# Other sizes of transfer at the layers' border, at the layers' last units and in w_down: two layers of cached attention and FFN on one core

## The chip, the core and the metric

The kernel runs on one core of a Trainium2 chip. The metric is the device time of one execution in microseconds, the median of several runs. A profile of one execution (engines, waits, DMA) goes with it.

The engines: PE multiplies matrices (its weight loads are told apart as PEld), DVE, ACT and POOL work on vectors, and SP issues all the loads here. Sixteen DMA engines move the data; each load is spread over all of them, and the loads of SP's queue are worked off in the order of their issue.

## What is computed

Twice, one after the other, an attention block and an FFN, each with a residual, for 4 rows of 512 (one new token in each of 4 sequences):

```python
def _A_ref(x, k_cache, v_cache, wq, wo):        # k_cache, v_cache: 4 x 8 x 8192 x 128
    q = (x @ wq).reshape(B, Sq, 32, 128).transpose(0, 2, 1, 3)
    k = jnp.repeat(k_cache, 4, axis=1)
    v = jnp.repeat(v_cache, 4, axis=1)
    p = softmax(jnp.einsum("bhqd,bhkd->bhqk", q, k) * 128 ** -0.5)
    o = jnp.einsum("bhqk,bhkd->bhqd", p, v)
    return o.transpose(0, 2, 1, 3).reshape(B, Sq, 32 * 128) @ wo

def _B_ref(x, w_gate, w_up, w_down):            # 512 x 1792, 512 x 1792, 1792 x 512
    return (silu(x @ w_gate) * (x @ w_up)) @ w_down

x = A_x
x = x + _A_ref(_layernorm(x), A_k_cache, A_v_cache, A_wq, A_wo)
x = x + _B_ref(_layernorm(x), B_w_gate, B_w_up, B_w_down)
x = x + _A_ref(_layernorm(x), A_k_cache, A_v_cache, A_wq, A_wo)
x = x + _B_ref(_layernorm(x), B_w_gate, B_w_up, B_w_down)
```

The caches are 64 MB each in bf16, and both layers read the same ones, so nearly all of the caches has to be fetched twice.

## The kernel before

**Units.** A unit is one of the 32 pairs of sequence and head group: a K and a V of 8192 x 128 in bf16, 2 MB each. They lie in `kv`, 8 slots of 2 MB in the on-chip memory (`kvf`, 128 partitions of 16 KB for a slot). A slot is used in eighths: `s6.3` is the name of the fourth 1024 columns of slot 6. For K an eighth is turned by DVE (`turn`) and multiplied on PE (`scores`, 4 matmuls); then the softmax, and `values` multiplies with V. The last unit of a layer has its V multiplied eighth by eighth (`block_last`, 8 matmuls each), all others in two blocks.

**Loads.** `items` is the order in which SP issues the loads; `pump` issues the next whenever its slot (`home`) is free. A usual unit is one DMA of 2 MB. Some units are loaded in quarters of 512 KB (`fours`, `part`): the last unit of each layer, whose V has a semaphore for each quarter (`split`, `sem_l`), and three units of layer 1 that come right behind the border. K and V of a unit have the same pieces, since the piece sets which keys lie in which partition. The last three units of layer 0 stay in their slots and are the first of layer 1.

**Border of the layers.** The FFN weights go where slots 6 and 7 were: `f0` is the first column of slot 6, then three pieces of w_gate (5376 columns), then w_down from `f1` (14 rows of blocks, `fo` = 0 to 13, of 512 columns each), then the last pieces of w_gate and w_up. The other pieces of w_up have room of their own. In the FFN of layer 0, the room of weights that were read is given to the K of two units of layer 1 (`ks[0]` into slot 6, `ks[1]` into slot 7), quarter by quarter: two quarters behind the gate matmuls, the others in the loop over `fo`, as soon as `fo` passes the quarter's end, and the last ones behind the loop. Then `heirs`: two of the kept K units hand their slots on, a quarter at a time, as their scores go on (`quarter`, called from `keys` and `finished`).

**Who waits for what.** There is no compiler that finds dependencies. Each instruction states names that it reads and writes, and `_Sync` keeps for each name its last writer and its readers (`_need`, `_record`, lines 42 to 93). A reader waits for the last writer of each name; a writer waits for the readers as well. For DMAs the writer is the semaphore that tells of the landing. For the weights, `at_w` gives the names: the eighths of slots 6 and 7 that the columns touch (`room`), and the block's own name.

```python
room = lambda a, b: places[(a - f0) // (TB * Dh):(b - 1 - f0) // (TB * Dh) + 1]
at_w = {"wg": room(f0, f0 + FR * F), "wg3": room(f2, f2 + F), "wu": room(f3, f3 + F),
        **{("wd", j): room(f1 + 2 * j * D, f1 + (2 * j + 2) * D) + [f"wd{j}"] for j in range(FO // 2)}}
```

**FFN.** `ffn` multiplies gate and up (56 matmuls each, the weights stationary, `w_sb[kt][:, f:f + 2 * P - 1:2]`: every second column), makes `hT` on DVE and ACT, then w_down. w_down is loaded in 7 blocks of 256 KB, two `fo` in each: a block is laid out so that a partition holds two neighbouring rows, and so gate and up take every second column. In layer 0 the w_down weights are stationary (4 matmuls for each `fo`, with a `warm` matmul before each pair, which does no needed work). In layer 1 `hT` is stationary and the weights stream (two matmuls for each `fo`), and nothing is given away. There the last load is w_down, behind the last V and w_gate; w_up and one piece of w_gate were kept from layer 0.

PE, DVE and ACT programs are taped first and then played with loops over the regular middle of each layer (`roll`); SP's is straight.

Of the kernel before, what the change touches and what calls it, by code (L numbers as in the profile page):

```python
# [146 lines left out]
def bass_interleave_layers__gqa_block_cached__swiglu_ffn__decode_kernel(  # L147
# [12 lines left out]
    B, _, D = A_x.shape  # L160
    _, G, S, Dh = A_k_cache.shape
# [4 lines left out]
    P = 128  # L166
    assert Dh == P and B * Hq == P and D % P == 0 and F % P == 0 and B == 4
    KT = D // P
    FO = F // P
# [23 lines left out]
    with ExitStack() as es:  # L193
# [16 lines left out]
        wg_sb = [kvf[:, a:a + F] for a in (f0, f0 + F, f0 + 2 * F, f2)]  # L210
        wu_sb.append(kvf[:, f3:f3 + F])
        wd_sb = kvf[:, f1:f1 + FO * D].rearrange("p (f n) -> p f n", f=FO)
        places = [f"s{s}.{q}" for s in range(NKEEP, NSLOT) for q in range(NB)]
        room = lambda a, b: places[(a - f0) // (TB * Dh):(b - 1 - f0) // (TB * Dh) + 1]
        at_w = {"wg": room(f0, f0 + FR * F), "wg3": room(f2, f2 + F), "wu": room(f3, f3 + F),
                **{("wd", j): room(f1 + 2 * j * D, f1 + (2 * j + 2) * D) + [f"wd{j}"] for j in range(FO // 2)}}
        wq_sb = sb("wq_sb", [P, KT, HqDh], BF16)
        wq_b = wq_sb[:].rearrange("p k n -> p (k n)").bitcast(U8)

# [43 lines left out]
        def few(ap):  # L263
# [10 lines left out]
        engines = {"pe": nc.tensor, "act": nc.scalar, "dve": nc.vector, "pool": nc.gpsimd, "sp": nc.sync}  # L274
        prog = {n: sem(f"prog_{n}") for n in engines}
        sem_s = [sem(f"sem_s{i}") for i in range(NSLOT)]
        sem_l = [sem(f"sem_l{q}") for q in range(NQ)]
        sem_h = [[sem(f"sem_h{k}{i}") for i in range(NQ)] for k in range(2)]
        sem_p = [sem(f"sem_p{i}") for i in range(7)]
        sem_x = sem("sem_x")  # L280
        sem_w = {n: [sem(f"sem_{n}{i}") for i in range(c)]
                 for n, c in (("wq", KT), ("wo", 1), ("wg", KT), ("wu", KT), ("wd", FO // 2))}
        sem_out = sem("sem_out")
        es.enter_context(nc.Block())
        T = _Sync(nc, engines, prog)
# [62 lines left out]
        split = {("V", L, unit_order[L][-1]) for L in range(2)}  # L348

        heirs = {("K", 1, unit_order[1][k]): items[ends[0] + 3 + k] for k in range(2)}  # L350
        fours = {(L, unit_order[L][-1]) for L in range(2)} | {(1, u) for u in unit_order[1][NRES:2 * NRES]}
        issued = [0]
        free = set(range(NSLOT))
        slot_of = {}
# [16 lines left out]
        def load_weight(name, i=0):  # L371
            if name == "wq":
                T.dma("sp", [(wq_sb[:, i, :], runs(A_wq[i * P:(i + 1) * P, :]))], sem_w["wq"][i], writes=[f"wq{i}"])
            elif name == "wo":
                n = G // 4
                w = REP * Dh
                T.dma("sp", [(wo_sb[:, g, :, :].rearrange("p e n -> p (e n)"), runs(A_wo[g * w:(g + 1) * w, :]))
                             for g in range(i * n, (i + 1) * n)], sem_w["wo"][0], writes=[f"wo{i}"])
            elif name == "wg":
                for k in range(KT - i):  # L380
                    T.dma("sp", [(wg_sb[k], runs(B_w_gate[k * P:(k + 1) * P, :]))], sem_w["wg"][k],
                          writes=(places if k == 0 else []) + [f"wg{k}"])
            elif name == "wu":
                for k in range(KT):
                    T.dma("sp", [(wu_sb[k], runs(B_w_up[k * P:(k + 1) * P, :]))], sem_w["wu"][k], writes=[f"wu{k}"])
            else:
                for j in range(FO // 2):
                    T.dma("sp", [(wd_sb[:, 2 * j:2 * j + 2, :].rearrange("p e n -> p (e n)"),
                                  runs(B_w_down[2 * j * P:(2 * j + 2) * P, :]))], sem_w["wd"][j], writes=[f"wd{j}"])

        def pump():
            while issued[0] < len(items):
                n = issued[0]
                it = items[n]
                if it[0][0] == "w":
                    if it[0] == "wg":
                        if not {NKEEP, NKEEP + 1} <= free:
                            return
                        free.difference_update((NKEEP, NKEEP + 1))
                    load_weight(*it)  # L400
                    issued[0] += 1
                    continue

                s = home(it)
                if s not in free:
                    return
                free.remove(s)
                kind, L, u = it
                slot_of[it] = s
                g, b = unit_gb(u)  # L410
                cache = A_k_cache if kind == "K" else A_v_cache
                if it in split:
                    n = NB // NQ
                    for q in range(NQ):
                        part(it, s, q * n, (q + 1) * n, sem_l[q])
                elif (L, u) in fours:
                    part(it, s, 0, NB, sem_s[s])
                else:
                    T.dma("sp", [(kv[:, s, :], runs(cache[b, g, :, :]))], sem_s[s], writes=[f"s{s}.{q}" for q in range(NB)])
                issued[0] += 1  # L420

        def part(it, s, a, b, sem_):
            kind, L, u = it
            assert (L, u) in fours
            n = NB // NQ
            w, m = n * TB * Dh, S // NQ
            src = (A_k_cache if kind == "K" else A_v_cache)[u % B, u // B, :, :]
            T.dma("sp", [(kv[:, s, q * w:(q + 1) * w], runs(src[q * m:(q + 1) * m, :])) for q in range(a // n, b // n)],
                  sem_, writes=[f"s{s}.{k}" for k in range(a, b)])

        def place(it, s):
            assert items[issued[0]] == it
            slot_of[it] = s
            issued[0] += 1

        def quarter(it, i):
            to = heirs[it]
            if i == 0:
                place(to, slot_of[it])
            n = NB // NQ  # L440
            part(to, slot_of[it], i * n, (i + 1) * n, sem_h[unit_order[1].index(it[2])][i])

        def finished(it):
            kind, L, u = it
            if (kind, 1, u) in kept and L == 0:
                slot_of[kind, 1, u] = slot_of[it]
                if kind == "K":
                    turned.update((1, u, q) for q in range(NB))
            elif it in heirs:
                quarter(it, NQ - 1)  # L450
                pump()
            else:
                free.add(slot_of[it])
                pump()
# [98 lines left out]
        def keys(L, u):  # L553
            def block(q):
# [6 lines left out]
                scores(L, u, q)  # L561
                if q == 0 and first:
                    deviation(lsc_sb, "lsc")
                if ("K", L, u) in heirs and (q + 1) % (NB // NQ) == 0 and q < NB - 1:
                    quarter(("K", L, u), q // (NB // NQ))
                if q == NB // NQ and L == 1 and first:
                    keep("wg")
                if q == NB - 1:
# [218 lines left out]
        def qkeep():  # L787
            T.op("dve", lambda e: e.tensor_copy(qr, ob4), reads=[f"pb{OUTB}"], writes=SCR)

        def kept_at(name, f=None):  # L790

            w = REP * Dh
            a = {"wg": 0, "wu": G - 1}[name] * w
            return a if f is None else wq_sb[:, f // w, a + f % w:a + f % w + 2 * P - 1:2]

        def park(name):

# [18 lines left out]
        def ffn(last):  # L816
# [3 lines left out]
            fb = lambda ap: ap.rearrange("p (f b) -> p f b", b=B)  # L820
            rb = rstd[:].unsqueeze(1).to_broadcast([P, FO, B])
            ks = items[ends[0] + 1:ends[0] + 3]
            n = NB // NQ
            size = n * TB * Dh
            for (w_sb, wname, bk) in ((wg_sb, "wg", gb), (wu_sb, "wu", ub)):
                out = bank(bk)[:, 0:WIDE // B * FO * B].rearrange("p (r f b) -> p f r b", f=FO, b=B)
                for kt in range(KT):
# [2 lines left out]
                    if bk == ub and kt and not last:  # L830
                        warm(3)
                    for fo in range(FO):
                        f = fo // 2 * 2 * P + fo % 2
                        w = kept_at(wname, f) if kt == FR and last else w_sb[kt][:, f:f + 2 * P - 1:2]
                        T.pe(out[:, fo, :, :], w, few(xn[:, kt * B:(kt + 1) * B]),
                             start=(kt + fo == 0), stop=(kt == KT - 1 and fo == FO - 1),
                             reads=[wname + "kept", "xn"] if kt == FR and last else
# [1 line left out]
                             writes=[f"pb{bk}"],  # L839
                             sig=(fo == FO - 1 and kt == KT - 1))  # L840
                if bk == gb and not last:
                    place(ks[0], NKEEP)
                    part(ks[0], NKEEP, 0, (f1 - f0) // size * n, sem_p[0])
            T.op("dve", lambda e: e.tensor_tensor(fb(gr), fb(gT), rb, ALU.mult),
                 reads=[f"pb{gb}", "rstd"], writes=["gr"])
            T.op("act", lambda e: e.activation(eg, gr, ACTF.Exp, scale=-1.0), reads=["gr"], writes=["eg"])
# [5 lines left out]
            if last:  # L852
# [11 lines left out]
                for fo in range(FO):  # L864
                    two = 2 if fo < BOTH and fo % 2 else 0
                    for i in (two, 1):
                        k, a, b = where[i]
                        T.pe(rows[i], hT[:, fo * B:(fo + 1) * B], wd_sb[:, fo, a:b],
                             start=(fo == i == 0), stop=(fo == (BOTH if i == 2 else FO) - 1),
                             reads=["hT"] + at_w["wd", fo // 2], writes=[f"pb{k}"], sig=(fo == (BOTH if i == 2 else FO) - 1))  # L870
                    if fo == BOTH - 1:
                        T.op("act", lambda e: e.activation(handed, rows[2], ACTF.Copy), reads=[f"pb{STEP}"], writes=["s0.0"])
                return rows
# [4 lines left out]
            for fo in range(FO):  # L878
                warm(2 if fo % 2 == 0 else 0, SBK[0])
                for nt in range(KT):  # L880
                    T.pe(out[:, nt, :, :], wd_sb[:, fo, nt * P:(nt + 1) * P], few(hT[:, fo * B:(fo + 1) * B]),
                         start=False, stop=(fo == FO - 1 and nt == KT - 1),
                         reads=["hT"] + at_w["wd", fo // 2], writes=[f"pb{OUTB}"], sig=(nt == KT - 1 and fo % 2 == 1))
                i = (f1 - f0 + (fo + 1) * D) // size
                if i > (f1 - f0 + fo * D) // size:

                    if i <= NQ:
                        part(ks[0], NKEEP, (i - 1) * n, i * n, sem_p[i - 2])
                        if i == NQ:
                            place(ks[1], NKEEP + 1)  # L890
                    else:
                        part(ks[1], NKEEP + 1, (i - NQ - 1) * n, (i - NQ) * n, sem_p[i - 2])
                        if fo == FO - 1:
                            part(ks[1], NKEEP + 1, (i - NQ) * n, (i - NQ + 1) * n, sem_p[5])
                            part(ks[1], NKEEP + 1, NB - n, NB, sem_p[6])


        def roll(name):
# [122 lines left out]
```

## Time and profile before

| | us |
|---|---|
| runs, median (lowest to highest of 3) | 644.43 (643.29 to 644.66) |
| the profiled execution's own time | 644.37 |
| its span, first to last instruction | 642.5 |
| PE busy in the span | 515.2 |
| DVE busy | 450.7 |
| ACT busy | 122.0 |
| moved by DMA | 273.30 MB, mean 425 GB/s |

How to read the rows that come: the 40 slices are equal parts of the span, 16.06 us each, and a digit is the busy share in tenths. In the chain of waits, and in an engine's order of time, a line gives the start and the length in microseconds, then who. A line of loads gives KB for each and the median time from the issue to the landing. A line of a group gives engine, operation, output and inputs, shapes and count, then busy us and mean ns of one, then the engine's idle time before it and what ended it. "Slowest" or "latest" DMA engine: a load has landed when all sixteen have done their part.

### The profile page before, as it was taken

How to read it: one execution, taken by the hardware profiler on the slowest of the kernel's cores; microseconds unless marked ns; L12 is line 12 of the kernel's file. 1: busy time of each engine (PE TensorE's matmuls, PEld its weight loads, DVE VectorE, ACT ScalarE, POOL GpSimd, SP SyncE). 2: the span in 40 equal slices, each digit the busy share in tenths (PEclk: the TensorE clock that was granted, in tenths of full speed). 3: DMA queues.
4: the chain of work that ended last, by engine and by line, in shares of the span. 5: the costliest groups of instructions: out<-in, count | busy, mean ns of one | idle time of the engine just before them, and what ended most of it. 6: DMA issues, size and time to landing. Idle time of an engine off the chain costs nothing.

```text
span 642.5 us, 13067 instructions
## 1 busy us (share of the span) xinstructions
PE 515.2 (80%) x5063; PEld 334.9 (52%) x5086; DVE 450.7 (70%) x1108; ACT 122.0 (19%) x401; POOL 19.3 (3%) x73
## 2 busy tenths in 40 slices
PE   1656797887979878797888889897868968988987
PEld 1424454554646545455556656564545535645655
DVE  2646666867867767768764759987776876758883
ACT  0111211212212212212221422221221221212222
POOL 0000000000000000000000000000000000000000
PEclk9977789978887897979998999998987989769799
DMA  8999999999999999999999999999999999999996
GB/s 351 433 423 428 440 431 428 435 433 435 429 437 430 433 430 437 429 435 430 433 419 420 423 435 429 430 436 428 433 433 439 428 430 433 439 428 433 424 430 287
DMA packets 12695, 273.30 MB, mean 425 GB/s; under 512 B 3032, under 2 KB 3040, under 8 KB 3040
## 3 DMA queue, kind: packets, MB, share of 16 engines
q1 hardware_dynamic: 12672, 272.98, 99.1%
q8 instruction: 16, 0.26, 0.2%
q14 instruction: 7, 0.06, 0.0%
HBM read 272.96 MB, written 0.00 MB: 425 GB/s over the span
## 4 chain that ended last, share of the span: by engine, by line
DMA 71%; PE 15%; DVE 9%; SPq 4%; issue 1%; ACT 0%; POOL 0%; DVEq 0%; POOLq 0%
DMA kvf<-in_A_k_cache_dram 57%; PE ps L100 15%; DMA kvf<-in_A_v_cache_dram 11%; DVE kvf L118 6%; SPq L136 4%; DMA kvf<-in_B_w_down_dram 2%; DVE acc L118 2%; DVE one L118 1%; DVE pT L118 0%; DVE m L118 0%; ACT pb L118 0%; POOL zq L492 0%; DVE oT L118 0%; ACT one L118 0%; SPq L134 0%
## 5 line engine op out<-in xcount | busy, mean ns | idle before, releaser
L118 DVE STREAM_TRANSPOSE kvf<-kvf 128x512 f32<-128x512 f32 x488 | 322.6, 686 | 87.1 <-DMA kvf<-in_A_k_cache_dram 87.1
L100 PE MATMUL ps<-kvf,zq 128*128 128x256 bf16 x2048 | 316.4, 297 | 16.6 <-DVE kvf L118 11.9
L100 PEld LDWEIGHTS ps<-kvf,zq 128*128 128x128 bf16 x2048 | 197.5, 108 | 78.3 <-DVE kvf L118 28.7
L118 ACT ACTIVATE pb<-m 1x128 f32<-1x128 f32 x64 | 19.7, 308 | 434.4 <-DVE m L118 434.1
L100 PE MATMUL ps<-kvf,pT 128*16 128x512 bf16 x992 | 66.6, 390 | 10.5 <-DVE rl L118 7.5
L118 DVE SCALAR_TENSOR_TENSOR acc<-ps,own,acc 128x128 f32<-128x128 f32 x186 | 65.2, 351 | 5.4 <-ACT acc L118 0.6
L100 PE MATMUL ps<-identf,one 128*1 128x128 f32 x64 | 17.6, 275 | 49.0 <-DVE one L118 48.8
L100 PEld LDWEIGHTS ps<-identf,one 128*1 128x1 f32 x64 | 5.1, 80 | 77.3 <-DVE one L118 72.9
L100 PEld LDWEIGHTS ps<-kvf,pT 128*16 128x16 bf16 x992 | 19.4, 89 | 40.0 <-issue 22.3
L118 DVE TENSOR_REDUCE one<-ps 128x1 f32<-128x256 f32 x64 | 26.0, 406 | 18.5 <-PE ps L100 18.3
L118 ACT ACTIVATE pb<-ps,one,rstd 128x256 bf16<-128x256 f32 x64 | 36.0, 563 | 2.1
L100 PEld LDWEIGHTS ps<-head,acc 128*128 128x128 f32 x124 | 21.5, 217 | 28.2 <-DVE acc L118 26.3
L492 POOL TENSOR_TENSOR zq<-scr,quad 128x64 bf16<-128x64 bf16 x62 | 18.1, 292 | 599.6 <-PE ps L100 478.5
L100 PE MATMUL ps<-head,acc 128*128 128x4 f32 x124 | 24.2, 266 | 14.8 <-DVE acc L118 14.7
L118 DVE RECIPROCAL rl<-ps 128x4 f32<-128x4 f32 x64 | 10.4, 163 | 35.4 <-PE ps L100 35.4
L100 PEld LDWEIGHTS ps<-one,pb 1*128 1x128 f32 x128 | 21.3, 207 | 26.3 <-ACT pb L118 22.8
L100 PE MATMUL ps<-one,pb 1*128 1x1 f32 x128 | 26.8, 276 | 9.1 <-ACT pb L118 9.1
L118 DVE STREAM_TRANSPOSE pT<-pb 128x256 bf16<-128x256 bf16 x64 | 26.0, 407 | 4.6 <-ACT pb L118 4.5
L100 PE MATMUL ps<-wq_sb 128*128 128x512 bf16 (+1 forms) x83 | 27.3, 399 | 2.0 <-issue 1.3
L100 PE MATMUL ps<-xn,wq_sb 128*128 128x32 bf16 x284 | 21.1, 181 | 6.6 <-DMA wq_sb<-in_A_wq_dram 6.0
L100 PEld LDWEIGHTS ps<-rsm,one 128*128 128x128 f32 x128 | 22.0, 215 | 4.0 <-ACT rsm L118 2.5
L100 PEld LDWEIGHTS ps<-o,wo_sb 128*128 (+1 forms) x256 | 19.7, 101 | 8.3 <-issue 4.6
(72 smaller groups left out, 254.7 us busy)
## 6 DMA issues: line engine op xcount, KB each, us to landing
kvf<-in_A_k_cache_dram SPq DMA_DIRECT2D x56, 2048.0 KB, 28.9
kvf<-in_A_v_cache_dram SPq DMA_DIRECT2D x56, 2048.0 KB, 32.7
kvf<-in_A_k_cache_dram SPq DMA_DIRECT2D x20, 512.0 KB, 8.4
kvf<-in_A_v_cache_dram SPq DMA_DIRECT2D x20, 512.0 KB, 11.6
wq_sb<-in_A_wq_dram SPq DMA_DIRECT2D x4, 1024.0 KB, 8.2
wo_sb<-in_A_wo_dram SPq DMA_DIRECT2D x8, 512.0 KB, 37.6
kvf<-in_B_w_down_dram SPq DMA_DIRECT2D x14, 256.0 KB, 18.3
kvf<-in_B_w_gate_dram SPq DMA_DIRECT2D x7, 448.0 KB, 17.9
```

The costliest lines, as they stand in the source:

```text
L100: return e.matmul(out, lhsT=lhsT if at is None else lhsT(place(at)), rhs=rhs, **kw)
L118: self.tape[engname].append((repr((name, args, kw)), lambda e, _: getattr(e, name)(*args, **kw), left, sig, None))
L136: ins = e.add_instruction(mybir.InstDMACopy(name=self.nc.get_next_instruction_name(), mode="Copy", queue="qSPDynamicHW", ins=e.lower_ap_dm ...
L492: T.op(eng, lambda e: e.tensor_tensor(dst, q4, m4_, ALU.mult), reads=keys_ + ["quad"], writes=["zq"])
```

## The change

- `pieces` takes the place of `fours`: a unit's pieces in eighths. Layer 0's last unit: (4, 2, 2), that is a half and two quarters; layer 1's last unit: (2, 2, 2, 1, 1); the three units behind the border: halves, (4, 4). Each piece is one DMA. For the last units' V each piece has its own semaphore.
- `quarter` becomes `succeed`: it issues a piece of the heir when the eighth that ends it was read.
- w_down is loaded in blocks `WD` of 4, 4, 4, 1 and 1 `fo`: three of 512 KB and two of 128 KB. So gate and up take every fourth column for the first 12 `fo`, neighbouring ones for the last two. `at_w` names the eighths that a whole block touches.
- `give(a, b)` issues the pieces of `ks[0]` and `ks[1]` whose end lies in columns a to b: once behind the gate matmuls, once for each `fo`, once behind the loop.

```diff
+        WD = [(0, 4), (4, 8), (8, 12), (12, 13), (13, 14)]
+        wd_of = lambda fo: next(j for j, (a, b) in enumerate(WD) if a <= fo < b)
...
-                **{("wd", j): room(f1 + 2 * j * D, f1 + (2 * j + 2) * D) + [f"wd{j}"] for j in range(FO // 2)}}
+                **{("wd", j): room(f1 + a * D, f1 + b * D) + [f"wd{j}"] for j, (a, b) in enumerate(WD)}}
...
-        fours = {(L, unit_order[L][-1]) for L in range(2)} | {(1, u) for u in unit_order[1][NRES:2 * NRES]}
+        pieces = {(0, unit_order[0][-1]): (4, 2, 2), (1, unit_order[1][-1]): (2, 2, 2, 1, 1),
+                  **{(1, u): (4, 4) for u in unit_order[1][NRES:2 * NRES]}}
...
-                for j in range(FO // 2):
-                    T.dma("sp", [(wd_sb[:, 2 * j:2 * j + 2, :].rearrange("p e n -> p (e n)"),
-                                  runs(B_w_down[2 * j * P:(2 * j + 2) * P, :]))], sem_w["wd"][j], writes=[f"wd{j}"])
+                for j, (a, b) in enumerate(WD):
+                    T.dma("sp", [(wd_sb[:, a:b, :].rearrange("p e n -> p (e n)"), runs(B_w_down[a * P:b * P, :]))],
+                          sem_w["wd"][j], writes=[f"wd{j}"])
...
                 if it in split:
-                    n = NB // NQ
-                    for q in range(NQ):
-                        part(it, s, q * n, (q + 1) * n, sem_l[q])
-                elif (L, u) in fours:
-                    part(it, s, 0, NB, sem_s[s])
+                    for i in range(len(pieces[L, u])):
+                        part(it, s, i, i + 1, sem_l[i])
+                elif (L, u) in pieces:
+                    part(it, s, 0, len(pieces[L, u]), sem_s[s])
...
+        def bounds(it, i):
+            n = pieces[it[1:]]
+            return sum(n[:i]), sum(n[:i + 1])
+
         def part(it, s, a, b, sem_):
...
+            w, m = TB * Dh, S // NB
+            at = [bounds(it, i) for i in range(a, b)]
+            T.dma("sp", [(kv[:, s, c * w:d * w], runs(src[c * m:d * m, :])) for c, d in at], sem_,
+                  writes=[f"s{s}.{k}" for c, d in at for k in range(c, d)])
...
+        def succeed(it, k):
+            to = heirs[it]
+            if to not in slot_of:
+                place(to, slot_of[it])
+            for i in range(len(pieces[to[1:]])):
+                if bounds(to, i)[1] == k + 1:
+                    part(to, slot_of[it], i, i + 1, sem_h[unit_order[1].index(it[2])][i])
...
-                if ("K", L, u) in heirs and (q + 1) % (NB // NQ) == 0 and q < NB - 1:
-                    quarter(("K", L, u), q // (NB // NQ))
+                if ("K", L, u) in heirs and q < NB - 1:
+                    succeed(("K", L, u), q)
...
+            rooms = [(k, NKEEP + n, i, n * SL + bounds(k, i)[1] * TB * Dh) for n, k in enumerate(ks)
+                     for i in range(len(pieces[k[1:]]))]
+
+            def give(a, b):
+                for n, (k, s, i, end) in enumerate(rooms):
+                    if a < end <= b:
+                        if i == 0:
+                            place(k, s)
+                        part(k, s, i, i + 1, sem_p[n])
...
-                        f = fo // 2 * 2 * P + fo % 2
-                        w = kept_at(wname, f) if kt == FR and last else w_sb[kt][:, f:f + 2 * P - 1:2]
+                        a, b = WD[wd_of(fo)]
+                        f, n = a * P + fo - a, b - a
+                        w = kept_at(wname, f, n) if kt == FR and last else w_sb[kt][:, f:f + n * (P - 1) + 1:n]
...
-                    place(ks[0], NKEEP)
-                    part(ks[0], NKEEP, 0, (f1 - f0) // size * n, sem_p[0])
+                    give(0, f1 - f0)
...
             for fo in range(FO):
                 warm(2 if fo % 2 == 0 else 0, SBK[0])
                 for nt in range(KT):
                     T.pe(out[:, nt, :, :], wd_sb[:, fo, nt * P:(nt + 1) * P], few(hT[:, fo * B:(fo + 1) * B]),
                          start=False, stop=(fo == FO - 1 and nt == KT - 1),
-                         reads=["hT"] + at_w["wd", fo // 2], writes=[f"pb{OUTB}"], sig=(nt == KT - 1 and fo % 2 == 1))
-                i = (f1 - f0 + (fo + 1) * D) // size
-                if i > (f1 - f0 + fo * D) // size:
-                    if i <= NQ:
-                        part(ks[0], NKEEP, (i - 1) * n, i * n, sem_p[i - 2])
-                        if i == NQ:
-                            place(ks[1], NKEEP + 1)
-                    else:
-                        part(ks[1], NKEEP + 1, (i - NQ - 1) * n, (i - NQ) * n, sem_p[i - 2])
-                        if fo == FO - 1:
-                            part(ks[1], NKEEP + 1, (i - NQ) * n, (i - NQ + 1) * n, sem_p[5])
-                            part(ks[1], NKEEP + 1, NB - n, NB, sem_p[6])
+                         reads=["hT"] + at_w["wd", wd_of(fo)], writes=[f"pb{OUTB}"], sig=(nt == KT - 1 and fo % 2 == 1))
+                at = f1 - f0 + fo * D
+                give(at, at + D)
+            give(at + D, 2 * SL)
```

## The prediction, made before the changed kernel was run

> **What bounds the kernel.** The page first: time is moved bytes.
>
> ```profile
> span 642.5 us, 13067 instructions
> ...
> DMA  8999999999999999999999999999999999999996
> GB/s 351 433 423 428 440 431 428 435 433 435 429 437 430 433 430 437 429 435 430 433 419 420 423 435 429 430 436 428 433 433 439 428 430 433 439 428 433 424 430 287
> ...
> DMA 71%; PE 15%; DVE 9%; SPq 4%; issue 1%; ACT 0%; POOL 0%; DVEq 0%; POOLq 0%
> ```
>
> The DMA row is 9 in every slice but the first and last. So a change counts by what it takes from the packets, by any stretch in which it leaves the 16 engines without work, and by what follows the last load. The change has three places: the border of the layers (about 316 to 370 us), the end (from 613) and the FFN. The chain of waits around the border, then PE's order of time there:
>
> ```profile
> 334.61 14.47 DMA kvf<-in_B_w_down_dram
> 349.12 0.59 PE ps L100 x9
> ```
>
> ```profile
> 346.18 0.35 PE L100 MATMUL ps<-scr,kvf 128*128 128x32 bf16 x8
> 346.38 0.38 PE L100 MATMUL ps<-wq_sb 128*128 128x512 bf16 x1
> 346.60 0.35 PE L100 MATMUL ps<-scr,kvf 128*128 128x32 bf16 x8
> ...
> 349.12 0.37 PE L100 MATMUL ps<-scr,kvf 128*128 128x32 bf16 x8 [0.51 <-DMA kvf<-in_B_w_down_dram]
> ```
>
> Eight matmuls are two fo of w_down; with a warm matmul a pair takes 0.42 us (346.18 to 346.60). The last block lands at 349.08, and pair 12, 13 starts behind it. SP's order of time, and single issues with their time to landing (issued 346.98, 349.52 and 354.23):
>
> ```profile
> 340.82 10.44 SPq L136 DMA_DIRECT2D kvf<-in_A_k_cache_dram  x8
> 353.35 3.52 SPq L136 DMA_DIRECT2D kvf<-in_A_v_cache_dram  x4
> ```
>
> ```profile
> kvf<-in_A_k_cache_dram SPq DMA_DIRECT2D x1, 512.0 KB, 6.8
> kvf<-in_A_k_cache_dram SPq DMA_DIRECT2D x1, 512.0 KB, 6.7
> kvf<-in_A_v_cache_dram SPq DMA_DIRECT2D x1, 512.0 KB, 6.9
> ```
>
> A quarter needs 1.23 us of all engines (landings in the trace: 352.57, 353.79, 355.02), so at the border some 5 us of work lie ahead of each issue. That is all the reserve there is.
>
> **The new wait.** ffn's places name the columns of slots 6 and 7 by 1024. Block 1 of the new w_down (fo 4 to 7) lies in columns 7424 to 9472 from f0, so its reads name s6.7, s7.0 and s7.1. give issues the second half of ks[0] behind fo 5 (8192 lies between 7936 and 8448), and that half writes s6.4 to s6.7. The matmul of fo 6, next on PE, reads s6.7 by name, and the last writer of s6.7 is now the K half under sem_p[1]. PE will wait for its landing, though no byte is shared. Before, fo 6 and 7 had a block of their own (8448 to 9472, s7.0 and s7.1), and no such wait.
>
> When it ends: block 1 lands where fo 6's block did (346.9), fo 4 and 5 take 0.25, the half is issued at some 347.3. It lands behind the same bytes as the quarter issued at 346.98, which landed 6.8 us later, at 353.8; 0.2 sooner for the larger packets ahead: 353.6. PE stands from 347.2 to 353.65 (a released matmul starts 0.05 later, as at 349.12). Behind the wait on PE lie fo 6 to 13, centering, q and the scores of layer 1; behind those, SP's issue of both halves of ks[1] (after fo 13) and the halves of the heirs. Four pairs: 353.65 + 3 × 0.42 = 354.90, and the issue follows a last pair's start by 0.40 (349.12 to 349.52): 355.3. For clock, the only like idle:
>
> ```profile
> 31.20:35.00 3.80, 0.00 (x1) 0.00 (x0) 0.00 (x0) 0.00 (x0) 0.29 (x1) 1.00 0.96 410
> 35.10:38.70 3.60, 0.00 (x0) 0.02 (x1) 1.18 (x4) 0.00 (x0) 0.00 (x0) 0.50 0.99 428
> 38.70:41.80 3.10, 3.09 (x23) 1.30 (x24) 2.31 (x5) 0.55 (x2) 0.00 (x0) 0.50 0.95 407
> 41.90:45.00 3.10, 3.10 (x27) 2.25 (x26) 3.03 (x8) 1.22 (x4) 0.00 (x0) 1.00 1.15 486
> ```
>
> These rows give PE, PEld, DVE, ACT, POOL, then the granted clock and the DMA share. After 7.5 us without matmuls (31.2 to 38.7) the clock is at half, and back 3.2 us after work begins. So the four pairs run at half clock, where a 512-wide warm matmul takes 588 against 376 ns (by form, 342.3 to 345.6): 0.2 more a pair, issue at 355.3 to 355.9; I take 355.7.
>
> Nothing else is queued on the DMA engines after 353.6 (ks[1] and the heirs all wait on PE). **Restart:** no row shows a 1 MB load into an empty queue in mid-kernel. The first load, issued at 0.74, has its first packets between 2.0 and 2.5 us, 1.3 to 1.8 later; the 4 KB of out, issued at 640.94, between 641.5 and 641.7, 0.6 to 0.8 later. I take 1.3, the near end of the like load: packets from 357.0, an idle of **3.4 us** on the latest engine (355.3 + 0.6 - 353.6 = 2.3 to 355.9 + 1.8 - 353.6 = 4.1). Engines that are ahead idle longer, but the end waits for the latest: at the end the DMA share falls by steps from 635 to 639.7, so they have that to give. The Trainium skill, "DMA: Bandwidth & Descriptors", section "Latency and other measured facts", states about 600 ns to the first byte of a hardware-issued DMA; by that restart the idle would be 2.7 and the time 0.7 lower, and only the row of out agrees with it.
>
> Next late: the first heir half, issued behind the fourth score block: 354.23 - 349.52 = 4.7 after the issue of fo 13, so 360.4, plus up to 1.7 if these 16 matmuls run at half clock (107 ns more each). ks[1] ends at 357.0 + 4.86 = 361.9; 360.4 + 1.3 = 361.7 just meets it, 363.4 misses it by 1.5. I take **0.3** (0 to 1.7). Later halves come at 4.2 us a unit on PE (the heirs' first issues, 353.35 and 357.57) against 4.86 on the DMA, so no third gap.
>
> **The other parts.** Packets: two 16 KB took 1.230 us on their engine, one of 32 KB 1.214; two of 8 KB 0.628. Six border loads save 4 × 0.016 each, 0.38; layer 0's last unit 0.06; layer 1's costs 0.05; w_down saves 0.05 a time (4 KB packets, not shown, estimated at half of 8 KB): **-0.5** in all (bounds 0 and -0.6), since the DMA is full elsewhere. SP issues 16 fewer DMAs at 0.59 us, at nothing: between bursts it waits for PE, and without that each would delay a landing by 0.59. Layer 0's V in halves waits one quarter longer for its first piece, at nothing: its last quarter (335.79) ends that stage.
>
> End: before, PE starts the last quarter's 16 matmuls at 632.09 behind a warm matmul of 631.73, 0.05 after the landing at 632.04. In eighths 8 of them (25 ns each) go ahead, but the flushed steps before them bind: **-0.1** (0 to -0.2). w_down's last block landed at 639.69 and PE was at it at 639.73, a tie; both move with the stream, and the new last block holds one fo: 0 (cover gone: one block's 0.6).
>
> **Weight step.** Gate and up now load stationary columns 8 bytes apart for 12 of 14 fo (before 4, now 2 for the rest): 96 loads in the last FFN, exposed.
>
> ```profile
> L100 PEld LDWEIGHTS ps<-kvf,pT 128*16 128x16 bf16 x992 | 19.4, 89 | 40.0 <-issue 22.3 <-DMA kvf<-in_A_v_cache_dram 4.1 <-DVE rl L118 0.2
> L100 PEld LDWEIGHTS ps<-xn,kvf 128*128 128x128 bf16 x196 | 5.8, 99 | 3.2 <-DMA kvf<-in_B_w_up_dram 2.3 <-issue 0.9
> L100 PEld LDWEIGHTS ps<-pT,kvf 128*128 128x128 bf16 x128 | 3.8, 96 | 2.8 <-DMA kvf<-in_A_v_cache_dram 2.0 <-issue 0.7
> L100 PEld LDWEIGHTS ps<-qg,identf 128*32 128x32 bf16 x256 | 3.4, 116 | 5.9 <-DVE qg L118 5.8
> ```
>
> Contiguous (pT) 96, 4-byte steps (xn,kvf) 99: nothing. The identity's columns, 8 bytes apart, take 116 for 32 against 89 for 16 contiguous. Bounds: 0, and 27 ns × 96 = 2.6. Such loads start every 25 ns while one lasts 97, so they overlap, and I take the end near the 4-byte row: **+0.1**. The Trainium skill, "SBUF — State Buffer", section "Door 1: The DMA port swizzle", says reads keep full rate with two hits in a 16-byte line; 8 bytes apart just has two, which would make this 0.
>
> **Sum.** 3.4 + 0.3 - 0.5 - 0.1 + 0.1 = +3.2 on the profiled execution's 644.37 (span 642.5 and 1.87 around it; the runs' median is 644.43): **647.6 us**.
>
> **Rivals.**
> (a) *No new dry spell*: the halves feed the border as the quarters did. This decides if the issue of ks[1]'s first half comes before 353.6 - 1.3 = 352.3, that is if fo 6 doesn't carry the wait. For it: no byte is shared, and the order before had none. Against: dependencies go by name, and part is called in the same round of the loop, ahead of fo 6. Then -0.5: 643.9, not slower. Chance 0.09.
> (b) *The border runs dry again and again*: PE stays at half clock through the first K unit of layer 1 (32 matmuls × 107 ns = 3.4 late), so heirs miss by 1.7 and the one after by 0.7. For it: a reserve of 0.2 us. Against: the clock came back after 3.2 us. 4.1 + 2.4 - 0.5 = +6.0: 650.4. Chance 0.13.
> (c) *The weight step costs its bound* on top of the forecast: +2.5, 650.1. For it the identity's row, against it the overlap. Chance 0.07.
>
> **Numbers.** Forecast 0.71. Its own bounds: 2.3 + 0 - 0.6 - 0.2 = +1.5 and 4.1 + 1.7 - 0.1 = +5.7; 645.9 to 650.1; with a run's scatter of some 0.2 below, and the ends above not likely together, 645.7 to 650.0, which takes in (b) and (c) in part; (a) is left out below. 0.2% is 1.3 us, about what a measurement here tells from no change. Faster than 643.1 only in (a) on a lucky run: 0.03. Within: the rest of (a) and a forecast at its very bottom, 0.09. Slower: 0.88.
>
> **What would show it.** A PE wait of about 6 us on a K load between 347 and 354 in the FFN of layer 0; DMA share near 0 for some 3 us around 355 and 9 elsewhere; K halves of ks[1] issued near 355.7 instead of 348 to 350.7; half clock after it. No 8-byte effect: gate and up matmuls of the last FFN still 25 ns apart. Wrong if PE goes from fo 5 to fo 6 without a wait, or if the stream has no gap.

## The result, and the profile after

| | us |
|---|---|
| changed kernel, median (lowest to highest of 5) | 652.32 (650.61 to 653.47) |
| kernel before, run beside it, median (5 runs) | 644.43 (643.29 to 644.73) |
| ratio of the times, 95% interval | 1.0121 (1.0101 to 1.0141) |
| profiled execution of the changed kernel: own time, span | 653.47, 651.7 |

Slower, as forecast, but by 7.9 us instead of 3.2: outside the range, whose upper end was 650.0. The profiled execution is the longest of the five; against the profiled one of before it is 9.1 longer.

The page of the changed kernel, its span, the rows of the 40 slices and the chain by engine:

```profile
span 651.7 us, 13049 instructions
...
DMA  8999999999999999999996999999999999999996
GB/s 348 436 429 417 447 423 438 430 434 432 429 436 424 440 428 436 433 432 434 422 422 262 351 431 430 430 429 436 431 432 432 432 430 436 430 432 434 425 427 283
...
DMA 65%; PE 18%; DVE 12%; SPq 2%; issue 1%; ACT 1%; DVEq 0%; POOL 0%; POOLq 0%
```

Before, every slice but the first and the last had a 9. Now slice 22 (342 to 358 us) has a 6, with 262 GB/s, and slice 23 still moves only 351. The chain's DMA share fell from 71% to 65%, and what it lost went to PE and DVE: at the border the stream no longer sets the pace. The rest of the rows is as before, so nearly all of the loss has one place. PE's waits there (total, times, longest), then the chain of waits and SP's order of time:

```profile
PE ps L100 <- DMA kvf<-in_A_k_cache_dram: 6.2, 1, 6.2
```

```profile
347.45 0.40 PE ps L100 x9
347.85 6.31 DMA kvf<-in_A_k_cache_dram
354.16 0.05 issue
354.21 1.67 PE ps L100 x26
355.88 0.22 issue
356.10 9.05 PE ps L100 x91
```

```profile
341.75 15.91 SPq L136 DMA_DIRECT2D kvf<-in_A_k_cache_dram  x4
363.35 2.29 SPq L136 DMA_DIRECT2D kvf<-in_A_v_cache_dram  x2
```

The forecast wait is there: fo 4 and 5 at 347.45, the issue of ks[0]'s second half at 347.85, its landing at 354.16, and fo 6 at 354.21. Then the four pairs, the last at 356.10, and SP's burst of four K halves ends there. So far each step is within 0.9 us of the prediction's numbers. What comes next is not. Single issues (size, us to landing), those of 347.85, 356.55 and 363.35, and the windows around them (length; PE, PEld, DVE, ACT, POOL busy; granted clock, DMA share, GB/s):

```profile
kvf<-in_A_k_cache_dram SPq DMA_DIRECT2D x1, 1024.0 KB, 6.3
kvf<-in_A_k_cache_dram SPq DMA_DIRECT2D x1, 1024.0 KB, 5.1
kvf<-in_A_v_cache_dram SPq DMA_DIRECT2D x1, 1024.0 KB, 5.1
```

```profile
351.00:354.00 3.00, 0.00 (x0) 0.00 (x0) 0.00 (x0) 0.00 (x0) 0.00 (x0) 0.50 0.41 175
354.00:357.00 3.00, 2.57 (x36) 1.62 (x38) 0.26 (x2) 0.00 (x0) 0.00 (x0) 0.50 0.00 0
357.00:360.00 3.00, 3.00 (x55) 1.92 (x56) 1.49 (x9) 0.22 (x1) 0.00 (x0) 0.50 0.71 273
360.00:363.00 3.00, 3.00 (x17) 2.18 (x16) 1.63 (x3) 2.84 (x6) 0.00 (x0) 0.50 0.99 426
363.00:366.00 3.00, 2.50 (x22) 1.86 (x21) 0.82 (x2) 1.28 (x3) 0.29 (x1) 0.95 0.62 180
```

Two things are to be seen. First, a half of 1 MB needs 5.1 us when it is issued into an empty queue (356.55) or a nearly empty one (363.35), where moving it takes 2.44 (the distance of two such landings when the queue is full, 374.76 and 377.20). Second, PE is back at 354.21, but the clock stays at 0.50 until 363.3. The first scores of layer 1 run at half speed, the first heir half is issued at 363.35, 6.8 us behind fo 13's issue (4.7 assumed), and the queue is dry a second time: 180 GB/s from 363 to 366, where the kernel before had 426:

```profile
363.00:366.00 3.00, 2.34 (x21) 1.80 (x20) 2.92 (x8) 1.70 (x6) 0.00 (x0) 1.00 1.01 426
```

By the landings the layer is 0.4 us late at the end of ks[0], 7.0 at the end of ks[1] (365.66 against 358.69), 8.7 at the end of the first heir's V (372.31 against 363.62), and no more than that at the last V of the kernel (8.6).

### The profile page after: what moved, and what is told of

Read it like the earlier page. It is cut to its first block, busy times and chain, and to the rows that moved or that the text cites. A ratio compares the mean times of both kernels' runs of the same rounds, so it can differ in the third digit from the quotient of the medians.

```text
span 651.7 us, 13049 instructions
## 1 busy us (share of the span) xinstructions
PE 520.2 (80%) x5063; PEld 338.0 (52%) x5086; DVE 451.1 (69%) x1108; ACT 122.0 (19%) x401; POOL 19.3 (3%) x73
## 4 chain that ended last, share of the span: by engine, by line
DMA 65%; PE 18%; DVE 12%; SPq 2%; issue 1%; ACT 1%; DVEq 0%; POOL 0%; POOLq 0%
DMA kvf<-in_A_k_cache_dram 53%; PE ps L100 18%; DMA kvf<-in_A_v_cache_dram 8%; DVE kvf L118 8%; DMA kvf<-in_B_w_down_dram 3%; SPq L136 2%; DVE acc L118 2%; DVE one L118 1%; DVE pT L118 1%; ACT pb L118 1%; DVE m L118 1%; ACT acc L118 0%; DVE oT L118 0%; POOL zq L502 0%; ACT one L118 0%
```

## The experiments

The theory after the result had three parts: A, the wait of fo 6 by name brings nearly all of the loss; B, within it, the empty queue restarts slower than assumed, and the half clock makes the heirs late, so that the queue empties again; C, the wider step of the weight columns costs something of its own. The rivals: the larger pieces feed the border worse with or without the wait; the loss is the restart alone, whatever the clock; the step costs nothing. "Before" is the kernel before on the same chip, in the same call; its median was 643.65 beside e1 to e4, 643.58 beside e5 to e8, and 644.38 beside e9 and e10.

**e1_own_names: the changed kernel without the wait.** fo 6 names only the eighths that its own columns touch.

```diff
-    reads=["hT"] + at_w["wd", wd_of(fo)], ...
+    reads=["hT", f"wd{wd_of(fo)}"] + room(f1 + fo * D, f1 + (fo + 1) * D), ...
```

> The changed kernel, but in the FFN of layer 0 a w_down matmul names only the eighths that its own 512 columns touch (and its block), not those of the whole block; loads and order stay. Theory A (the name s6.7 alone makes PE wait 6.5 us, and all the loss at the border follows from it): the wait and the gaps of the DMA are gone, and what is left is -0.5 us of packets, -0.1 at the last V, and +0.6 for the stationary columns 8 bytes apart (33 instead of 25 ns a load in the last FFN): 644.4, within 0.2% of before. Rival B (halves at the border are too coarse by themselves): the DMA still runs dry between 352 and 372, 647 to 650.

Measured: 644.87, ratio 1.0011 (1.0002 to 1.0021). PE waits for no K load at the border, and the stream has a dent and no hole. The window of e1 that answers to the dry one:

```profile
348.00:351.00 3.00, 2.50 (x47) 1.66 (x47) 0.87 (x6) 0.00 (x0) 0.00 (x0) 1.00 0.93 344
```

So, by the ratios, 7.1 of the 7.8 us hang on one name in one list of reads, not on the size of the pieces; 0.7 us (0.1 to 1.4) is left for all the rest of the change.

**e2_wait_only: the kernel before, with the wait.** Its quarters and blocks stay; fo 6 reads the last eighth of slot 6 as well.

```diff
-    reads=["hT"] + at_w["wd", fo // 2], ...
+    reads=["hT"] + at_w["wd", fo // 2] + ["s6.7"] * (fo == 6), ...
```

> The kernel before with one name more: the matmuls of fo 6 in layer 0's FFN also read s6.7. All sizes are those of before. Theory A: the wait alone costs most of the loss; quarters are issued earlier behind it (the first one of the second K behind fo 9, the heirs' first behind two score blocks instead of four), so somewhat less than the changed kernel: 649 to 651. Rival B (halves do the harm, the wait is mostly covered by quarters): 645 to 647.

Measured: 650.29, 1.0104 (1.0086 to 1.0122). PE's wait in e2:

```profile
PE ps L100 <- DMA kvf<-in_A_k_cache_dram: 7.1, 1, 7.1
```

The wait alone brings 6.7 us, with none of the larger pieces. Together, e1 and e2 settle A: necessary and nearly sufficient.

**e3_warm_wait: the changed kernel, PE kept busy in its wait.** 28 needless matmuls of 512 columns ahead of fo 6.

```diff
-    warm(2 if fo % 2 == 0 else 0, SBK[0])
+    warm(58 if fo == 6 else 2 if fo % 2 == 0 else 0, SBK[0])
```

> The changed kernel with 28 more warm matmuls of 512 columns ahead of fo 6, some 6.0 us that fill PE's wait; they compute nothing needed. Theory A with the clock as its second half (half clock from 349.6 to 363.3 delays the heirs' issue to 6.8 us behind fo 13, where the trace before has 4.7): full clock, the issue behind fo 13 some 0.6 earlier, the second gap nearly gone, 649.0 to 650.0. If the clock doesn't matter and the gaps come from the sizes: 652.3 as the changed kernel.

Measured: 649.93, 1.0095 (1.0077 to 1.0112). PE's order of time at the wait, then two windows of e3:

```profile
346.14 0.37 PE L100 MATMUL ps<-scr,kvf 128*128 128x32 bf16 x8
346.36 6.42 PE L100 MATMUL ps<-wq_sb 128*128 128x512 bf16 x28
353.05 0.36 PE L100 MATMUL ps<-scr,kvf 128*128 128x32 bf16 x8 [0.27 <-DMA kvf<-in_A_k_cache_dram]
```

```profile
352.00:355.00 3.00, 2.68 (x41) 1.41 (x39) 0.26 (x2) 0.00 (x0) 0.00 (x0) 1.00 0.00 0
355.00:358.00 3.00, 2.55 (x59) 2.08 (x61) 1.74 (x9) 0.47 (x1) 0.00 (x0) 1.00 0.95 306
```

The clock is 1.00 throughout, the first heir half comes 4.7 us behind fo 13's issue, as in the prediction, and the dry stretch of 3 us is there all the same. By the ratios 1.7 us of the loss go with the clock and 6.1 stay; the two intervals (from 1.0101 up, and up to 1.0112) just overlap.

**e5_wait_second and e6_wait_first: a shorter wait.** As e2, with `"s6.5"` or `"s6.3"` in the place of `"s6.7"`: fo 6 waits for an earlier quarter of ks[0], and more quarters lie ahead in the queue when it is released.

> The kernel before with one name more, as e2, but fo 6 waits for the quarter before (s6.5, landing some 1.2 us sooner than s6.7). Theory A (the loss is a gap whose length is landing, plus PE's way to the next issue, plus the restart of an empty queue, less the bytes still queued): PE goes on 1.2 sooner while the queue ends at the same time, so the gap is 1.2 shorter, and the later gaps shorter too: 1.2 to 2.5 less than e2, 647.8 to 649.1. Rival C (any wait on a load at this place costs about the same, by the half clock alone): 650.

> The same with s6.3, the first two quarters, issued ahead of w_down's end: they land some 2.4 us sooner than s6.7. Theory A: 2.4 us of bytes are still queued when PE goes on, and the next issue follows 1.2 later, with a restart of 2.2 to 2.7: a gap of about 1 to 1.5 us and little after it, 645 to 646.5. Rival C: 649 to 650.

Measured: e5 648.41, 1.0069 (1.0053 to 1.0084), as expected. e6 648.67, 1.0064 (1.0048 to 1.0081): two to four microseconds more than expected, and no better than e5 although PE was released 1 us sooner. One window of e5, then three of e6:

```profile
354.00:357.00 3.00, 2.79 (x62) 1.81 (x59) 1.25 (x9) 0.00 (x0) 0.00 (x0) 0.83 0.92 300
```

```profile
357.00:360.00 3.00, 3.00 (x16) 2.13 (x16) 1.31 (x3) 2.82 (x6) 0.00 (x0) 0.50 1.04 382
360.00:363.00 3.00, 2.50 (x23) 1.88 (x20) 1.03 (x3) 0.98 (x2) 0.29 (x1) 0.97 0.77 208
363.00:366.00 3.00, 3.00 (x28) 2.40 (x25) 2.97 (x7) 1.41 (x5) 0.00 (x0) 1.00 0.79 300
```

The first gap shrank, to 2.2 us by the table below (1 to 1.5 expected). But the half clock lasted until 360.2, longer than in e5 (355.0), so the first V quarter of an heir was issued 5.1 us behind fo 13's issue (4.0 in e5, 3.8 before), and a second dry stretch followed, 208 GB/s. That made the clock the suspect for the second stretch, and e9 its test.

**e9_first_warm and e10_wait_warm: e6 and e2 with PE kept busy.** `warm(44 ...)` in e6, `warm(64 ...)` in e2 ahead of fo 6.

> The kernel before with the wait of fo 6 on the first K quarter (as in e6_wait_first, 648.67 beside 643.65) and 22 needless matmuls of 512 columns (0.213 us each, 4.7 us) on PE inside that wait, so that PE is not idle in it. This tells what brought e6's second dry spell (358 to 366 us). Theory A, the half clock that followed the wait did it: full clock throughout, the first V quarter of an heir issued some 4.0 to 4.3 us behind fo 13's issue instead of 5.1, no second dry spell or a slight one, and 645 to 646.5 us. Theory B, the second dry spell comes from the late queue alone whatever the clock: the dip at 358 to 366 stays and the time is 648 to 649.

> The kernel before with the wait of fo 6 on the last K quarter (as in e2_wait_only, 650.29 beside 643.65) and 32 needless matmuls of 512 columns (6.8 us) on PE inside that wait of 7.1 us. Theory A, the wait costs some 4.5 us by the empty queue itself and half clock costs the rest, as the changed kernel lost 2.4 us when its own wait was filled: clock 1.0 throughout, heirs 4.0 to 4.3 us behind fo 13's issue, 647.5 to 648.5 us. Theory B, the clock matters only for the changed kernel's larger pieces: 650 to 650.5 us.

Measured: e9 646.63, 1.0039 (1.0025 to 1.0054). The same stretch of e9:

```profile
357.00:360.00 3.00, 2.50 (x23) 1.92 (x21) 1.19 (x4) 2.77 (x7) 0.29 (x1) 1.00 0.93 366
360.00:363.00 3.00, 3.00 (x28) 2.41 (x26) 2.97 (x7) 1.39 (x5) 0.00 (x0) 1.00 0.98 399
```

Full clock, the heir's quarter 3.8 us behind fo 13's issue, and no second dry stretch: in these two executions, with the same wait, the half clock had made it. e10: 649.59, 1.0081 (1.0064 to 1.0098), 5.2 us over before, more than the 4 to 5 expected by theory A and less than theory B has. By the ratios filling the wait bought 1.5 us in e2, 1.6 in e6 and 1.7 in the changed kernel; all three go the same way, but in each pair the intervals overlap. In the profiled executions, of e2 the shortest of four (649.34) and of e10 the longest (649.84), it bought nothing. The landings of these executions say why. The first three columns of the table give how far the last landing of three loads lies behind the last landing of ks[0], in each profiled execution, less the same distance in the kernel before (4.90, 9.83, 14.75). The fourth is the time from PE's release to the first issue of an heir, the last the lead that this issue has over the last landing of ks[1] (5.3 before).

| | ks[1] | heir's V | heir's K | release to heir | lead |
|---|---|---|---|---|---|
| changed kernel (halves) | +6.6 | +8.3 | +8.3 | 9.1 | 2.3 |
| e3, clock kept (halves) | +5.5 | +5.8 | +6.3 | 6.3 | 4.0 |
| e2, wait for the last quarter | +5.5 | +5.9 | +5.9 | 6.5 | 3.7 |
| e10, clock kept | +5.6 | +5.6 | +5.6 | 5.4 | 4.9 |
| e5, wait for the third quarter | +3.6 | +5.2 | +5.2 | 6.3 | 3.2 |
| e6, wait for the second quarter | +2.2 | +5.1 | +5.1 | 7.4 | 2.0 |
| e9, clock kept | +3.0 | +3.0 | +3.5 | 5.4 | 4.8 |

The first column is the first dry stretch. With the wait on the whole of ks[0] it is 5.5 us in e2 and e3, 5.6 in e10 and 6.6 in the changed kernel. In the two rows with halves it holds more than the stretch, though. In the changed kernel fifteen of the sixteen DMA engines had reported ks[1] by 364.12, and the last one did so at 365.66; in e3 the times are 362.19 and 363.43. A packet of 16 KB from the instruction queue, 0.93 us long, starts shortly ahead of each (363.64 and 360.35). The trace does not name the engine of a packet, so that this packet held up that one engine is likely and not shown. Counted by the fifteenth report of each load, in all kernels, the first stretch costs 5.1 us in the changed kernel and 4.4 in e3, and the second 3.2 and 1.4; the sums stay.

The step to the second column is the second dry stretch, and it goes with the lead: nothing at 4.8 and 4.9, 0.3 and 0.4 at 4.0 and 3.7, then 1.6 (e5), 1.7 (the changed kernel) and 2.8 (e6) at 3.2 to 2.0. By the fifteenth report it goes with the lead too: nothing in e9 and e10, 0.9 in e2, 1.4 in e3 and e5, 2.9 in e6, and 3.2 in the changed kernel, whose lead is then 0.8. The half clock takes the lead away: from the release to the heir's issue it costs 1.0 us in e2 and 0.9 in e5, 2.0 in e6 and 2.8 in the changed kernel, against the kernels with the clock kept. In e2 the rest of the lead was nearly enough, and so e10 had little to win there.

Each row is one execution. One of e6's four took 646.65, 2.0 less than their median; how long its half clock lasted is not known. And e9's first stretch is 0.8 longer than e6's, for a reason that was not sought.

**e4_two_fo, e7_wide_step, e8_last_pieces: the rest of the change.** e4 is the changed kernel with w_down in the old seven blocks of two fo, so that the step between columns is 4 bytes and no wait arises. e7 has the new w_down blocks (8 bytes for 12 of 14 fo) with each fo's own names and all pieces in quarters. e8 has blocks of two fo and two of one, quarters at the border, and the last units' new pieces.

```diff
+ WD = [(fo, fo + 2) for fo in range(0, FO, 2)]                      # e4
+ pieces = {(L, unit_order[L][-1]): (2, 2, 2, 2) for L in range(2)} | {(1, u): (2, 2, 2, 2) for u in unit_order[1][NRES:2 * NRES]}   # e7
+ WD = [(fo, fo + 2) for fo in range(0, 12, 2)] + [(12, 13), (13, 14)]   # e8
```

> The changed kernel with w_down in seven blocks of two fo as before; halves at the border and the new pieces of the last units stay. Theory A: no block straddles s6.7 and slot 7 while it is being given away, so no wait, and the weight step is 4 bytes again (25 ns a load): -0.4 us of packets and -0.1 at the end, 643.9. Against e1 it gives the price of the wide step by itself: 0.6 us less. Rival B: as in e1, 647 to 650.

> w_down in the new blocks (4, 4, 4, 1, 1 fo), names of a matmul's own columns, and all loads of units in quarters as before. So the weight step of 8 bytes is nearly alone. By the trace of the changed kernel (33 ns a weight load where it was 25, 112 loads in the last FFN; last V to the end 11.03 us where it was 10.45) +0.6 to +0.9, less 0.1 of packets: 644.3 to 644.6 beside a before of 643.7. If the halves and not the step made e1 slower than e4: 643.6.

> What is left of the change without its costs: w_down in blocks of two fo, the last two single; layer 0's last unit in a half and two quarters, layer 1's with eighths at its end; the border in quarters as before. No new wait, no wide step. -0.1 us of packets and -0.1 to -0.2 at the end: 643.5 beside a before of 643.7, which the runs can't tell from no change. If the pieces at the end matter more than the last landings say: 643.0 or less.

Measured: e4 643.79, 0.9997 (0.9987 to 1.0007); e7 645.01, 1.0018 (1.0009 to 1.0027); e8 644.36, 1.0002 (0.9993 to 1.0011). The groups of gate's and up's weight loads on the pages of the changed kernel and of e4 (busy us, mean ns), and then the last 42 of their matmuls at the end, in PE's order of time, in the changed kernel and before:

```profile
L100 PEld LDWEIGHTS ps<-xn,kvf 128*128 128x128 bf16 x196 | 7.1, 116 | 2.5 <-DMA kvf<-in_B_w_up_dram 1.7 <-issue 0.9
```

```profile
L100 PEld LDWEIGHTS ps<-xn,kvf 128*128 128x128 bf16 x196 | 5.7, 97 | 3.1 <-DMA kvf<-in_B_w_up_dram 2.2 <-issue 0.9
```

```profile
645.66 1.51 PE L100 MATMUL ps<-xn,kvf 128*128 128x32 bf16 x42
```

```profile
636.85 1.20 PE L100 MATMUL ps<-xn,kvf 128*128 128x32 bf16 x42
```

With steps of 8 bytes a load takes 116 ns instead of 97 and the next starts every 33 ns instead of 25, in the changed kernel, e1 and e7 alike, and not in e4 and e8. In the tail of the changed kernel the 84 matmuls with these loads take 0.6 us longer (1.04 + 0.59 + 1.51 against 0.85 + 0.50 + 1.20), and all 112 of gate and up, with those whose weights were kept, 0.8 (643.65 to 647.55 against 635.22 to 638.33). From the last V's landing to the end e7 takes 11.4 us, before 10.45; but single executions scatter here, for e5 with the old step takes 11.15. e7's ratio makes the step 1.2 us (0.6 to 1.7), somewhat over what was expected.

e4 and e8 can't be told from before: neither the halves at the border, nor the other pieces of the last units, nor the blocks of one fo bring anything that this measurement shows. No version tried beats the kernel before.

## Why the prediction was right and wrong

**Right: the mechanism, its place and its sign.** The wait of fo 6 on a K half that shares no byte with it, by the name s6.7: predicted from 347.2 to 353.65, found from 347.9 to 354.2. The issue behind fo 13 was put at 355.7 and came at 356.55, the four pairs at half clock all through (0.61 to 0.64 us a pair instead of a mix with 0.42). Rival (a) is ruled out by the changed kernel and shown in e1, where the name is gone and the gap with it.

**Wrong, first: the restart of the empty queue**, in the term of 3.4 us. The step reads "I take 1.3, the near end of the like load", for the time from the issue to the first packets, and then counts the half at its normal pace. The half took 5.14 us from issue to landing, which is 2.7 over its moving time of 2.44; in e3 it took 5.08. Its packets came 1.3 to 2.4 us after the issue, so 1.3 was right for the first engines alone, and those that came first took 1.8 to 1.9 us each instead of the 1.21 of a steady queue. The first packet of every engine was done 3.1 to 3.6 us after the issue, where 1.3 and 1.21 make 2.5. With the issue 2.39 behind the landing (2.1 assumed) ks[1]'s first half lands 5.1 late instead of 3.4. Of these 1.7 us, 0.3 are the later issue, 1.0 the slow first packets, and 0.4 the way from the last packet's end (361.32) to the landing (361.69), which a count from a landing to a first packet leaves out. At full clock, in e3, the half still lands 4.3 late. In the changed kernel ks[1]'s second half lands 1.5 later again, but by the one engine that is told of below the table, so this is not shown to be the restart. The like load, issued at 0.74 in the kernel before, had the whole price in its row, and only its first packets were taken:

```profile
wq_sb<-in_A_wq_dram SPq DMA_DIRECT2D x1, 1024.0 KB, 5.0
```

The Trainium skill has a rule nearer than the one that the prediction weighed: "SBUF — State Buffer", section "The DMA setup-cost knee (why "@ 1 MiB" ≠ asymptote)", gives each transfer a fixed 2 us or so and fits 2 + bytes / 436 GB/s, by which an estimate for this half is 4.4 us. The trace shows 5.1.

**Wrong, second: "Next late: the first heir half ... I take 0.3".** This rests on the clock coming back after 3.2 us, as it had before. It came back 9.1 us after PE resumed, the heir half was issued 6.8 us behind fo 13 instead of 4.7, and the second dry stretch cost 1.7 by the landings and 3.2 by the fifteenth reports, so that by these it is the larger part of the miss. That is rival (b), which had a chance of 0.13: half clock into the first K unit of layer 1, and heirs that come too late. It held for about half of the unit: 28 score matmuls took 4.54 us instead of 3.27, not the 3.4 late that (b) has for all 32. Its price of 2.4 for the later gaps lies between the two counts; it fell short, at 650.4, for the first reason. e9 and e3 show that the clock brings most of this stretch: with PE kept busy nothing of it is left in e9, and in e3 0.3 by the landings or 1.4 by the fifteenth reports.

**Wrong, third: the weight step, "I take the end near the 4-byte row: +0.1".** The argument was that loads overlap. They do, but the interval grows too, from 25 to 33 ns: 0.8 us in the tail of the changed kernel by the matmuls alone, 1.2 (0.6 to 1.7) by e7. It lies inside the bounds of 0 to 2.6, at neither end. The prediction's sign for it ("still 25 ns apart") failed plainly, and so did the rule drawn from the Trainium skill, "SBUF — State Buffer", section "Door 1: The DMA port swizzle": two hits in a 16-byte line did not keep the full rate here.

**Not to be resolved: packets -0.5 and end -0.1.** e4 has the halves and the last units' pieces without wait or wide step and stands at -0.2 us (-0.8 to +0.5), e8 at +0.1 (-0.5 to +0.7). Both terms fit, and so does nothing. The part of e1 beyond before, 0.7 us, is covered by the weight step.

**The sum as it came**, in the profiled execution: 0.4 us late ahead of the wait, 8.3 for the two stretches, and 0.6 more behind the last V (11.0 us to the end against 10.45), where the weight step lies. That is 9.3 beside the measured 9.1. The 7.9 between the medians is less; the other four executions took 650.61 to 652.44 and were not traced. The range failed because its bounds held the issue at 355.9 and the restart at 1.8 at most, the latter from one load's first packets and not from the whole load, and left the clock to a rival.

## What to carry to other kernels

A name that covers more than an instruction touches turns a hand-over of space into a wait; when the blocks of a load change, go through the names of every reader against every write that is issued just ahead of it. Where a queue of loads is fed by the engine that waits, price the gap as a whole load into an empty queue, issue to landing (the kernel's first load shows it), and then ask what clock that engine has when it has to feed the queue again. If such a wait can't be avoided, needless matmuls in it won back some 1.7 us of 7.8 here, by ratios whose intervals just overlap.

## What the runs showed of the hardware

- **An empty queue restarts slowly.** 1 MB: 5.0 us for the kernel's first load, 5.08 and 5.14 at the border, from issue to landing, against 2.44 of moving; a quarter of 512 KB: 3.4 to 3.5 us against 1.23, with the queue empty (e2, e10) and still 3.4 to 3.5 with a last quarter under way that landed up to 1.5 us after the issue (e5, e6, e9). Why the first packets are slow was not tried.
- **The half clock lasts in steps of some 3.4 us.** It held 13.7 us in the changed kernel (349.6 to 363.3), 10.2 in e6 (350.0 to 360.2), 6.8 in e5 (348.2 to 355.0) and 6.8 in e2 (351.1 to 357.9): four, three, two and two times 3.4. The Trainium skill, "TensorE: Matmul & The Clock Gate", section "What's actually happening", has a free-running window of 3.4 us and full clock after at least one busy window. The steps agree; that one is enough was not so in two of the four: in the changed kernel and in e6 a whole step in which the records show PE busy was not enough. Those steps held centering, q and the first scores; the one that sufficed in e5 held w_down's pairs with their wide warm matmuls, the one in e2 some of both. Whether that decides was not tried.
- **A step of 8 bytes in a weight load costs**, 116 against 97 ns a load and 33 against 25 ns between starts; a step of 4 bytes does not (97 to 99, against 96 for contiguous columns).
